# Seven block products for eight in the gate products of a fused attention and GLU kernel

## Chip, cores and metric

One core of one Trainium2 chip. The time is device microseconds (us) of one execution of the whole kernel; several runs are given by their median. Engines as the profile names them: PE is TensorE (matmuls), PEld its weight loads, DVE is VectorE, ACT is ScalarE, POOL is GpSimd, SP is SyncE, which issues most transfers. PSUM is the memory that PE writes to, in 8 banks; DVE and ACT read it, Pool does not. SBUF is the working memory.

## What is computed

Attention over chunks, chosen by bounds, for 4 batches of 8 heads, 768 positions and 64 dimensions; its output, laid out as 3072 tokens by 512, goes through a gated feed-forward layer (FFN) of 1536 columns:

```python
    # attention: for each query the top 6 chunks of 32 keys by an upper bound, causal
    scores = scale * np.matmul(q, k.transpose(0, 1, 3, 2))
    scores = np.where(mask, scores, -1000000000.0)
    ...
    attn = attn / (np.sum(attn, axis=-1, keepdims=True) + 1e-09)
    return np.matmul(attn, v).astype(np.float32)

    # FFN: x [3072, 512], w_gate and w_val [512, 1536], w_out [1536, 512]
    gate = 1.0 / (1.0 + np.exp(-(x @ w_gate)))
    val = x @ w_val
    return (gate * val @ w_out).astype(np.float32)
```

The sigmoid is computed as tanh of half the argument: (tanh(g/2) + 1) times v, with the factor 0.5 put in at the very end.

## The kernel before

The 3072 tokens are handled in eight units of 384 (`units`, u0 to u7), each of three blocks of 128 tokens. For each unit the kernel prepares keys and queries, bounds the chunks (`choose`, tiles `ub`, `ubn`, `mx`, `ap`, `apt`), computes scores (`sc`, L896), their exponentials on ACT (`exp`, L907), the causal mask on Pool (`cm`, L913), the product with the values (`pv`, L929), and turns the result into `xT`, a tile of 4 blocks of 128 input rows by 384 tokens. Then `ffn` (L1062) takes it through the FFN:

- 12 blocks of 128 FFN columns (`fb`). For each, a gate product `g` and a value product `v` (L1078): 4 matmuls each, one for each block of 128 input rows, that stream 384 tokens. ACT takes the tanh (`gate`, L1087) and DVE makes `hg` = (gate + 1) x v (L1091).
- Units 0 to 3 multiply `hg` by w_out as it is (`o`, L1119; `osb`, the output staging). Units 4 to 7 (`PAIRED`) do it in `pair` (L989): a product of 2 x 2 blocks by seven block products in place of eight (Strassen's scheme in Winograd's form), with sums of `hg` blocks (`sw`, `sx`, L1000) and of w_out blocks (`tw`, L984) on DVE and Pool, the products `p1` to `p7` (L1013) on PE, and sums out of PSUM on DVE (L1030). `held` keeps the third token block of an even unit until the odd unit's third block joins it (`u45`, `u67`).

Each step is added to a `Plan` by name, with its dependencies, the engines that may run it and an estimate of its cost. The order in which each engine gets its instructions, and which engine takes which step, is not decided when the kernel is built: it is written out in the string `ORDER` (`name=engine`, P for PE, A for ACT, V for DVE, G for Pool, S for SP), and the buffers in the string `SLOTS` (`name:slot`). Engines run their own instructions in that order; between engines only the dependencies hold. All PSUM tiles take one of 8 slots, so a product waits until the last reader of the former tile of its slot is done.

Loads of q, k, v go by SP's queue; w_gate (`wg0` to `wg2`), w_val (`wv`) and w_out (`wo`) go by Pool's queue, in thirds of 0.5 MB, between Pool's other instructions:

```python
    def weights(i, prio, after):
        lo, hi = 512 * i, 512 * i + 512
        return plan.add(f"wg{i}", {POOL: (760, 760)}, lambda e: nc.gpsimd.dma_start(wg16[:, :, lo:hi], wgs[:, :, lo:hi]),
                 reads=after, writes=[("wg", i)], prio=prio, dma=(3000, 2048)), ...
```

At the start, `first` handles block 0 of the batches (`kf`, `qf`, `vf`, `scf`, `attf`, `pvf`, `xf`, `xpsf`), `load_wide` brings the keys and queries of u1 and u2 (`kq_u`), and copies of a pattern (`epat`, steps `hkp`) fill parts of the key tiles `hk`.

Of the kernel before, what the change touches and what calls it, by code (L numbers as in the profile page):

```python
# [100 lines left out]
cmf_1_0=G k0_u1=S kn_u1_0=G kT_u1_0=P vf_1=S vf1_1=G vc_1=A pvf_1_0=P rzf_1_0=V xf_1_0=V vf1_2=G cmf_1_1=G xpsf_0_1=P pvf_1_1=P
rzf_1_1=V xf_1_1=V kf16_2=A scf_2=P xpsf_0_0=P xpsf_1_0=P ap0=V kx1_u1_2=V vf_2=S vc_2=A wg0=G wv0=G xpsf_1_1=P expf_2_0=A
cmf_2_0=G pvf_2_0=P ap1=V rzf_2_0=V kt_u1_0=V xf_2_0=V expf_2_1=A cmf_2_1=G pvf_2_1=P k1_u1=S q1_u1=S q2_u1=S qn_u1_2=A xTf_0_1=A
kn_u1_1=A kT_u1_1=P q0_u1=S k3_u1=S q3_u1=S qn_u1_1=G wv1=G kn_u1_3=G xTf_1_0=A xTf_0_0=A hkp110=A qn_u1_3=G xpsf_2_0=P qT_u1_2=P
hq1=V rzf_2_1=V xf_2_1=V xTf_1_1=V kx1_u1_0=V hk0_u1_0=V xpsf_2_1=P xTf_2_1=V kx1_u1_1=V wg1=G qn_u1_0=A xTf_2_0=A kt_u1_1=A
kcr_f=G wv2=G qf_u1_2=V qm_u1_2=G kT_u1_3=P qT_u1_1=P qf_u1_1=A hq1_u1_1=A kx0_u1_3=V qT_u1_3=P qf_u1_3=V kx1_u1_3=V qT_u1_0=P
qf_u1_0=V hk0_u1_2=G qm_u1_3=G kx0_u1_1=V kx0_u1_0=V kcr_u1=V hk1_u1_1=A qm_u1_1=A qm_u1_0=A wg2=G kt_u1_3=V hk1_u1_3=V hkf0=V
hq0_u1_2=V g_u0_3=P g_u0_0=P g_u0_2=P tanh_u0_3=A tanh_u0_2=A hq0_u1_3=A hkp101=A hq0_u1_0=A g_u0_1=P ub_u1=P ubn0_u1=V ubm0_u1=V
hq0=V mx0_u1=V ap0_u1=V apt0_u1=V hqm0_u1_0=G v_u0_0=P v_u0_2=P v_u0_3=P hg_u0_3=V wo0=G hkp111=G ubn1_u1=V tanh_u0_0=A hq0_u1_1=A
tanh_u0_1=A hg_u0_0=V v_u0_1=P hg_u0_1=V hg_u0_2=V v_u0_7=P v_u0_4=P hqm0_u1_2=A sc_u1_0_2=P exp_u1_0_2=A sc_u1_2_2=P sc_u1_2_0=P  # L110
sc_u1_0_1=P sc_u1_2_1=P exp_u1_0_1=A v_u0_5=P g_u0_5=P tanh_u0_5=A hq1_u1_0=V kcr1=V hk0_u1_3=V hg_u0_5=V g_u0_7=P tanh_u0_7=A
wo1=G hk0_u1_1=G hq1_u1_2=G hkf1=G hk1_u1_0=G hq1_u1_3=G exp_u1_2_1=A g_u0_4=P tanh_u0_4=A hg_u0_7=V ubm1_u1=V mx1_u1=V ap1_u1=V
apt1_u1=V sc_u1_3_2=P exp_u1_3_2=A exp_u1_2_2=A exp_u1_2_0=A cm_u1_2=G sc_u1_1_0=P sc_u1_1_2=P sc_u1_3_1=P exp_u1_1_2=A v_u0_6=P
sc_u1_0_0=P sc_u1_3_0=P g_u0_6=P exp_u1_3_1=A exp_u1_1_0=A tanh_u0_6=A exp_u1_3_0=A hg_u0_4=V hg_u0_6=V sc_u1_1_1=P v_u0_9=P
v_u0_8=P v_u0_10=P g_u0_10=P tanh_u0_10=A exp_u1_1_1=A hg_u0_10=V g_u0_9=P tanh_u0_9=A g_u0_11=P tanh_u0_11=A exp_u1_0_0=A
g_u0_8=P tanh_u0_8=A v_0_3=S wo2=G cm_u1_3=G hqm1_u1_2=G v_0_1=S v16_0_1=G v_0_2=S v16_0_3=G v16_0_2=G pv_u1_3=P pv_u1_2=P
# [242 lines left out]
def kernel(  # L359
# [10 lines left out]
    nc = tc.nc  # L370
# [19 lines left out]

    plan = Plan(
# [3 lines left out]
    )  # L395

# [665 lines left out]
    def ffn(u, base, span):  # L1062
# [4 lines left out]
        for fb in range(NFB):  # L1067
# [3 lines left out]
            if fb % 2 == 0:  # L1071
                hgs.append(Buf("hg", f"hg_{u.name}_{fb // 2}", [128, 2, T], F16))
# [185 lines left out]
```

## Time and profile before

| | us |
|---|---|
| median of 3 runs | 289.97 |
| lowest, highest | 289.52, 290.89 |
| the profiled execution, its own time | 288.62 |
| its span in the profile | 286.6 |

The span goes from the first to the last instruction that the profile records; the profiled execution's own time has what lies around it too. A row of the grouped views reads: line, engine, operation, what it writes <- what it reads, the shapes, the count | busy us, mean ns of one | idle time of the engine just before, and what ended it. In a timeline a row begins with start and length in us, and the bracket at its end is idle time of that engine before it with what released it. Matmuls are pipelined, so the length of one matmul overlaps the next; the distance of the starts is what it takes of PE.

Two more rows of the profile, its waits of the longest total (engine, line, what it waited for: us in total, times, longest):

```profile
ACT gate_u L1087 <- PE g_u L1078: 53.1, 44, 8.3
POOL sw L1000 <- DVE hg_u L1091: 30.8, 5, 8.2
```

### The profile page before, as it was taken

To read this page: it belongs to the slowest core of one execution; us is meant where nothing else is said; L and a number is where in the kernel's file an instruction comes from. 1 tells how busy PE (TensorE), PEld (TensorE's weight loads), DVE (VectorE), ACT (ScalarE), POOL (GpSimd) and SP (SyncE) were. 2 spreads that over 40 slices of the span, in tenths; PEclk is the share of its full clock that TensorE was granted. 3 is DMA by queue.
4 is the path that set the end of the run, shared out by engine and by line. 5 is a ranking of instruction groups with operands and counts; after the bars stand their busy time and mean duration, and the time that the engine had idled before them with its cause. 6 is when DMAs were issued, how large, how long until landed. Compare 5 with 4: busy or idle time off the path is not lost.

```text
span 286.6 us, 7277 instructions
## 1 busy us (share of the span) xinstructions
PE 272.8 (95%) x2764; PEld 186.3 (65%) x2764; DVE 212.3 (74%) x615; ACT 186.9 (65%) x392; POOL 148.2 (52%) x233
## 2 busy tenths in 40 slices
PE   3878999999999999999999999999999999999994
PEld 2654566667755765556677548767876786676673
DVE  3678846687999989796989997866725756373785
ACT  5688578779976965369999769997763402514210
POOL 6567773768394803926677765655611080130430
PEclk9999999999999999999999999999999999999999
DMA  7999999999999994799950030000020020000124
GB/s 166 238 221 195 196 204 223 249 174 204 175 206 188 163 193 104 160 162 243 173 113 2 0 113 2 2 0 2 2 77 0 1 75 0 2 0 0 68 81 183
DMA packets 123377, 32.69 MB, mean 114 GB/s; under 512 B 111440, under 2 KB 120400, under 8 KB 123344
## 3 DMA queue, kind: packets, MB, share of 16 engines
q1 hardware_dynamic: 118592, 27.53, 45.9%
q0 software_dynamic: 4752, 4.72, 9.8%
q8 instruction: 21, 0.34, 0.5%
q14 instruction: 12, 0.10, 0.1%
HBM read 30.67 MB, written 6.29 MB: 129 GB/s over the span
## 4 chain that ended last, share of the span: by engine, by line
PE 81%; DMA 12%; SPq 2%; POOL 1%; DVE 1%; issue 1%; DVEq 0%
PE g_u L1078 19%; PE v_u L1078 19%; PE sc_u L896 11%; PE o_u L1119 10%; PE p_u L1013 9%; PE pv_u L929 6%; DMA wo<-in_moe_w_out_dram 5%; DMA wg<-in_moe_w_gate_dram 4%; PE ube_u L835 2%; DMA kq_u<-in_q_dram 2%; PE xps_u L956 1%; SPq L586 1%; DMA kf<-in_k_dram 1%; SPq L575 1%; DVE ox L1030 1%
## 5 line engine op out<-in xcount | busy, mean ns | idle before, releaser
L907 ACT ACTIVATE att_u<-sc_u 128x512 f16<-128x512 f32 (+3 forms) x184 | 86.8, 570 | 5.0 <-PE sc_u L896 2.5
L1087 ACT ACTIVATE gate_u<-g_u 128x384 f16<-128x384 f32 x96 | 47.1, 503 | 58.4 <-PE g_u L1078 53.1
L1091 DVE SCALAR_TENSOR_TENSOR hg_u<-gate_u,v_u 128x384 f16<-128x384 f16 x96 | 50.8, 543 | 36.0 <-PE v_u L1078 20.9
L1078 PE MATMUL g_u<-xT_u,wg 128*128 128x384 f16 x384 | 73.2, 326 | 0.9 <-DMA wg<-in_moe_w_gate_dram 0.9
L1078 PE MATMUL v_u<-xT_u,wv 128*128 128x384 f16 x384 | 72.5, 326 | 0.0
L1078 PEld LDWEIGHTS <-wg 128*128 128x128 f16 x384 | 36.0, 98 | 24.5 <-DMA wg<-in_moe_w_gate_dram 1.8
L1078 PEld LDWEIGHTS <-wv 128*128 128x128 f16 x384 | 36.2, 98 | 22.9 <-issue 0.5
L913 POOL TENSOR_SCALAR_AFFINE_SELECT att_u<-att_u 128x384 f16<-128x384 f16 (+1 forms) x56 | 28.2, 514 | 36.1 <-ACT att_u L907 30.6
L1119 PE MATMUL o_u<-wo,hg_u 128*128 128x512 f16 x144 | 34.6, 379 | 0.4 <-DMA wo<-in_moe_w_out_dram 0.3
L929 PE MATMUL pv_u<-v,att_u 128*128 128x65 f16 x640 | 26.6, 193 | 0.0
L929 PEld LDWEIGHTS <-att_u 128*128 128x128 f16 x640 | 24.5, 98 | 2.2
L896 PE MATMUL sc_u<-hqo,hko 128*128 128x128 f16 (+2 forms) x220 | 25.7, 243 | 0.0
L896 PE MATMUL sc_u<-hqe,hke 128*128 128x128 f16 (+2 forms) x220 | 25.1, 243 | 0.0
L1119 PEld LDWEIGHTS <-hg_u 128*128 128x128 f16 x144 | 13.5, 98 | 13.9 <-issue 0.6
L612 POOL CAST v<-v 128x512 f16<-128x512 f32 x23 | 13.7, 613 | 15.0 <-DMA v<-in_v_dram 14.7
L896 PEld LDWEIGHTS <-hke 128*128 128x128 f16 x220 | 16.7, 98 | 5.3 <-ACT xT_u L407 0.6
L896 PEld LDWEIGHTS <-hko 128*128 128x128 f16 x220 | 16.2, 98 | 4.3 <-DVE hqo L409 0.2
L636 POOL TENSOR_SCALAR qm_u<-qf_u 128x768 f32<-128x768 f32 (+3 forms) x10 | 16.2, 1617 | 3.3 <-PE ubo_u L835 2.0
L1030 DVE SCALAR_TENSOR_TENSOR sw<-p_u,sw 128x256 f32<-128x256 f32 (+1 forms) x20 | 10.6, 529 | 6.1 <-PE p_u L1013 5.7
L948 DVE TENSOR_TENSOR x_u<-pv_u,rz_u 128x384 f16<-128x384 f32 (+1 forms) x28 | 14.5, 525 | 0.4
L858 DVE MAX8 mx_u<-ubn_u 128x8 f32<-128x8 f32 (+16 forms) x152 | 12.6, 159 | 0.3
L1128 ACT ACTIVATE osb_u<-o_u 128x512 f32<-128x512 f32 x10 | 6.0, 596 | 10.1 <-PE o_u L1119 10.1
(159 smaller groups left out, 442.5 us busy)
## 6 DMA issues: line engine op xcount, KB each, us to landing
v<-in_v_dram SPq DMA_DIRECT2D x23, 256.0 KB, 4.4
k<-in_k_dram SPq DMA_DIRECT2D x12, 384.0 KB, 5.5
q<-in_q_dram SPq DMA_DIRECT2D x12, 384.0 KB, 5.5
out_dram<-osb_u SPq DMA_DIRECT2D x12, 256.0 KB, 3.4
out_dram<-sw SPq DMA_DIRECT2D x8, 256.0 KB, 2.0
wg<-in_moe_w_gate_dram POOLq DMA_DIRECT2D x3, 512.0 KB, 11.5
wv<-in_moe_w_val_dram POOLq DMA_DIRECT2D x3, 512.0 KB, 11.2
wo<-in_moe_w_out_dram POOLq DMA_DIRECT2D x3, 512.0 KB, 13.2
```

Source lines behind the costliest of these rows:

```text
L612: plan.add(f"v16_{b}_{ib}", {POOL: pool(H * D)}, lambda e: nc.gpsimd.tensor_copy(v16[b % 2][:, ib, :, 0:D], at(t)), reads=[t], writes=[("v ...
L636: (nc.vector if e == DVE else nc.gpsimd).tensor_scalar_max(o, i, 0.0)
L896: nc.tensor.matmul(at(t)[:, o:o + 128 * m], hk[b % 2][e_][:, p, 128 * jb:128 * jb + 128], hq[u.side][e_][:, p, 128 * x:128 * (x + m)], sta ...
L907: plan.add(f"exp_{u.name}_{h}_{y}", {ACT: act(n)}, lambda e, t=t, att=att, b0=b0, n=n: nc.scalar.activation(at(att)[:, b0:b0 + n], at(t), ...
L913: nc.gpsimd.affine_select(out=dv, in_=dv, compare_op=ALU.is_ge, fill=0.0, base=0, pattern=[[0, u.m], [1, 128]], channel_multiplier=-1)
L929: nc.tensor.matmul(at(pv)[:, last, x, :], at(att)[:, c:c + 128], v16[b % 2][:, jb, h, :], start=(jb == 0), stop=(jb == ib))
L948: plan.add(f"x_{u.name}_{p}", {DVE: dve(u.t)}, lambda e: nc.vector.tensor_tensor(at(x_).rearrange("p a (e d) -> p e a d", e=2), at(pv)[:, ...
L1013: nc.tensor.matmul(at(to)[:, side], a(j)[:, i], b(j)[:, i], start=j == i == 0, stop=j == 2 and i == 1)
L1078: nc.tensor.matmul(at(t), w16[:, c, 128 * fb:128 * fb + 128], at(u.xt)[:, c, :], start=(c == 0), stop=(c == 3))
L1087: plan.add(f"tanh_{u.name}_{fb}", {ACT: act(T)}, lambda e, g=g, gate=gate: nc.scalar.activation(at(gate), at(g), AF.Tanh, scale=0.5), read ...
L1091: plan.add(f"hg_{u.name}_{fb}", {DVE: dve(T)}, lambda e, w_=w_, gate=gate, hg=hg, fb=fb: nc.vector.scalar_tensor_tensor(at(hg)[:, fb % 2], ...
L1119: nc.tensor.matmul(at(o), at(hgs[fc // 2])[:, fc % 2, 128 * tb:128 * tb + 128], wo16[:, fc, lo:hi], start=(fc == 0), stop=(fc == NFB - 1))
```

## The change

The gate products of units 5, 6 and 7 are changed for four of the six pairs of FFN column blocks: pairs 1 to 4, so blocks 2 to 9. A pair's product of 512 input rows by 256 columns with 384 tokens is cut into 2 x 2 blocks each way (input rows 256 + 256, columns 128 + 128, tokens 192 + 192) and done by seven block products for eight. Each block product is 2 matmuls of 192 tokens.

- `sums_of` adds, once for each pair, four sums of w_gate blocks (`ss0` to `ss3`, kept in slots of the `v` tiles) and, for each of the three units, four sums of `xT` blocks (`tt0` to `tt3`, kept in parts of the key and query tiles that are no longer needed).
- `by7` adds the seven products into four PSUM tiles (`p1`, `p26`, `p53`, `p74`), a move of `p1` to SBUF (`m1`), and six sums into two f32 tiles `f0` and `f1` of 384 tokens each, from which the tanh reads. For pairs 1, 3 and 4 (`SLOW7`) three moves (`m26`, `m53`, `m74`) first bring the products to SBUF (`tm`), so that the sums may run on Pool or DVE; for pair 2 the sums read PSUM and run on DVE. A moved tile takes one of two places in a key tile.
- Value products, the other gate products and the w_out products stay as they were.
- `ORDER` and `SLOTS` are new from their first entries; 24 of the 1826 steps go, 223 come, and 148 of the steps that stay run on another engine. In the plan, unit 5's FFN is added after unit 6's attention, and the estimates for `qm` on Pool are raised.

```diff
@@ ORDER, SLOTS @@
-ident=G v10=G ident16=V k2_u1=S kn_u1_2=A kT_u1_2=P epat0=V epat=G hkp010=V hkp011=A hkp100=A kcr0=V hkp000=G kf1_0=S kf0_0=S
...
+k2_u1=S ident=G epat0=V epat=G hkp010=A ident16=V hq1=V kcr0=V kn_u1_2=V kT_u1_2=P kt_u1_2=A kx1_u1_2=V kf1_0=S kf0_0=S kfT_0=P
...
@@ the planner's estimates of qm on Pool @@
-POOL: pool(2.2 * u.n)
+POOL: pool(3 * u.n)
-POOL: pool(4.6 * u.n)
+POOL: pool(6 * u.n)
@@ before ffn @@
+    SLOW7 = {(u, "g", i) for u in (5, 6, 7) for i in (1, 3, 4)}
+    BY7 = {u: {("g", i) for i in (1, 2, 3, 4)} for u in (5, 6, 7)}
...
+    def sums_of(u, next_):
...
+                w, out_ = blocks_of(m, i), ss[m, i]
+                for n, (a, b, op) in enumerate(((lambda w=w: w(1, 0), lambda w=w: w(1, 1), ALU.add), (out_[0][1], lambda w=w: w(0, 0), ALU.subtract),
+                                                (lambda w=w: w(0, 0), lambda w=w: w(1, 0), ALU.subtract), (lambda w=w: w(0, 1), out_[1][1], ALU.subtract))):
+                    plan.add(f"ss{n}_{m}{i}", {DVE: dve(256, 2), POOL: pool2(256)}, ...
...
+        for n, (a, b) in enumerate(((lambda: x_(0, 1), lambda: x_(0, 0)), (lambda: x_(1, 1), lambda: t_(0)),
+                                    (lambda: x_(1, 1), lambda: x_(0, 1)), (lambda: x_(1, 0), lambda: t_(1)))):
+            plan.add(f"tt{n}_{u.name}", {DVE: dve(384, 2), POOL: pool2(384)}, ...
...
+    def by7(u, m, i, next_, views):
...
+        f = [Buf("np", f"f{y}_{name}", [128, 2, 192]) for y in range(2)]
+        slow = (u.i, m, i) in SLOW7
...
+                for c in range(2):
+                    nc.tensor.matmul(at(to)[:, side], a()[:, c], b()[:, c], start=c == 0, stop=c == 1)
...
+        product("p1", p1, 0, lambda: w(0, 0), lambda: x_(0, 0), [])
+        product("p2", p26, 0, lambda: w(0, 1), lambda: x_(1, 0), [])
+        product("p6", p26, 1, s7[1][1], lambda: t_(1), tk(1))
+        product("p5", p53, 0, s7[0][1], lambda: t_(0), tk(0))
+        product("p3", p53, 1, s7[3][1], lambda: x_(1, 1), [s7[3][0]])
+        product("p7", p74, 0, s7[2][1], lambda: t_(2), tk(2))
+        product("p4", p74, 1, lambda: w(1, 1), lambda: t_(3), [(f"tt{u.i}", 3)])
...
+        def move(p, src, dst, n, reads, writes):
+            plan.add(f"{p}_{name}", {ACT: act(192 * n), DVE: dve(192 * n)}, lambda e: copy(e, dst(), at(src)), ...
+        move("m1", p1, lambda: v_(2), 1, [p1], [q[2]])
+        if slow:
+            tmp = Buf("tm", f"tm_{name}", [128, 3, 2, 192])
+            move("m26", p26, ...
+            move("m53", p53, ...
+            move("m74", p74, ...
...
+        def onto(p, n, src, dst, other, reads, writes):
+            plan.add(f"{p}_{name}", {POOL: pool2(192 * n), DVE: dve(192 * n)} if slow else {DVE: dve(192 * n)}, lambda e: both(e).tensor_tensor(
+                dst(), src[0](), other(), ALU.add), ...
+        onto("c11", 2, a26, lambda: v_(0, 2), lambda: v_(2).to_broadcast([128, 2, 192]), [q[2]], [q[0], q[1]])
+        onto("c4", 1, a5, lambda: v_(3), lambda: v_(1), [q[1]], [q[3]])
+        onto("c3", 1, a7, lambda: v_(2), lambda: v_(1), [q[1]], [q[2]])
+        onto("c12", 1, a3, lambda: v_(1), lambda: v_(3), [q[3]], [q[1]])
+        onto("c22", 1, a7, lambda: v_(3), lambda: v_(3), [q[3]], [q[3]])
+        onto("c21", 1, a4, lambda: v_(2), lambda: v_(2), [q[2]], [q[2]])
@@ ffn @@
+            seven = [u.i in BY7 and (m, fb // 2) in BY7[u.i] for m in "gv"]
...
+                if seven[0]:
+                    gs = by7(u, "g", fb // 2, next_, views)
...
+            if seven[0]:
+                _, gv, gk = gs[fb % 2]
+            else:
+                g = ps(f"g_{u.name}_{fb}", "ff", [128, T])
...
+            plan.add(f"tanh_{u.name}_{fb}", {ACT: act(T, not seven[0])}, lambda e, gv=gv, gate=gate: nc.scalar.activation(
+                at(gate), gv(), AF.Tanh, scale=0.5), reads=gk, writes=[gate], prio=next_(EV))
@@ the units' sequence @@
     attend(units[5], 5.0)
-    ffn(units[5], 6.0, 0.95)
...
     attend(units[6], 6.0)
+    ffn(units[5], 6.0, 0.95)
     ffn(units[6], 7.0, 0.95)
```

More of the change, by code (lines that the diff above doesn't have):

```diff
@@ L101 @@
[L101 to L104, printed above, removed]
```

576 lines of the change are left out of this document (334 added, 242 removed), and 2 rows, old and new, of the table plan.

## The prediction

> **What bounds the kernel now.** I read first the page's busy times and its row of granted clocks, then the busy time of each engine in four stretches (the columns are the stretch, its length, then each engine's busy us with its instructions in brackets, the granted clock, the DMA share and GB/s).
>
> ```profile
> span 286.6 us, 7277 instructions
> PE 272.8 (95%) x2764; PEld 186.3 (65%) x2764; DVE 212.3 (74%) x615; ACT 186.9 (65%) x392; POOL 148.2 (52%) x233
> ...
> PEclk9999999999999999999999999999999999999999
> ```
>
> ```profile
> 0.00:60.00 60.00, 50.70 (x466) 33.25 (x467) 40.49 (x127) 43.96 (x93) 38.23 (x71) 1.00 1.08 210
> 80.00:100.00 20.00, 20.00 (x193) 12.00 (x192) 19.16 (x56) 16.27 (x37) 14.83 (x22) 1.00 1.00 185
> 200.00:270.00 70.00, 70.00 (x613) 49.99 (x611) 39.71 (x101) 27.69 (x61) 19.59 (x32) 1.00 0.04 16
> 270.00:287.00 17.00, 12.10 (x99) 9.32 (x96) 11.55 (x27) 2.13 (x5) 3.98 (x6) 1.00 0.37 139
> ```
>
> PE is idle for 286.6 - 272.8 = 13.8 us, of which 60 - 50.70 = 9.3 us lie in the first 60 us and 17 - 12.10 = 4.9 us at the end. Between 200 and 270 us it has no gap while DVE is busy 57%, ACT 40% and Pool 28% of the time. A busy PE need not be PE at its peak, so next I took runs of equal matmuls out of the chain of waits (start, length, what):
>
> ```profile
> 206.49 0.91 PE pv_u L929 x30
> ...
> 217.56 1.95 PE v_u L1078 x12
> ...
> 228.06 2.62 PE p_u L1013 x24
> ```
>
> 384 columns take 1.95/12 = 162.5 ns, 256 take 109.2 ns, 65 take 30.3 ns: a straight line, 0.416 ns a column and 2.7 to 3.3 ns for each matmul. The page counts as many weight loads as matmuls, 2764 each, so a fresh load for every matmul is hidden even behind 65 columns. PE streams at its rate, and in this stretch only fewer columns, or a wait, can move the end. The timeline shows where it does wait late, and its last matmuls:
>
> ```profile
> 277.83 0.39 PE L1013 MATMUL p_u<-wo,held 128*128 128x256 f16 x2 [0.70 <-DVE held L409]
> ...
> 281.99 0.82 PE L1013 MATMUL p_u<-tw,hg_u 128*128 128x256 f16 x6
> ```
>
> One wait of 0.70 us, and 286.6 - 282.8 = 3.8 us for the last sums and store.
>
> **The change part by part.**
>
> *Fewer columns on PE.* Four pairs in each of three units are 12 pairs. Each loses 8 matmuls of 384 columns (8 x 162.5 = 1300 ns) and gets 7 products of 2 matmuls of 192 columns. No row shows 192; the line puts it between the 256 and the 65 columns at 162.5 - 192 x 0.416 = 82.6 ns, and 14 x 82.6 = 1156 ns. The saving is 144 ns a pair, 1.73 us in all. Nothing covers PE, so this counts in full if PE stays fed. The Trainium skill, "TensorE: Matmul & The Clock Gate", section "Back-to-back issue gap", speaks against it: it gives about 81 ns for a matmul of 128 columns and 131 ns for 512 in a real stream of loads and matmuls. On a line between these two, an estimate from that page, a pair would go from about 8 x 114 to 14 x 89 ns and the change would cost 4 us. The trace disagrees: 384 columns take 162.5 ns and 65 take 30.3 ns, each with its load.
>
> *What the other engines get.* Counted in the listing of the changed kernel: 27 two-block moves out of PSUM and 12 one-block moves, 72 sums, 16 weight sums (256 columns) and 12 input sums (384 columns). Of the 72 sums 28 stand on Pool and 44 on DVE, so "most on Pool" does not hold as listed. Prices:
>
> ```profile
> L1030 DVE SCALAR_TENSOR_TENSOR sw<-p_u,sw 128x256 f32<-128x256 f32 x12 | 5.1, 423 | 2.9 <-PE p_u L1013 2.5
> ...
> L1000 DVE TENSOR_TENSOR sw<-hg_u,sw 128x256 f16<-128x256 f16 x6 | 1.7, 282 | 0.0
> L409 DVE COPY qf_u<-qT_u 128x384 f32<-128x384 f32 x3 | 1.6, 546 | 0.4 <-PE qT_u L734 0.4
> ```
>
> ```profile
> L1087 ACT ACTIVATE gate_u<-g_u 128x384 f16<-128x384 f32 x96 | 47.1, 503 | 58.4 <-PE g_u L1078 53.1 <-DVE hg_u L1091 3.0 <-DVE ubn_u L851 1.7
> ```
>
> ```profile
> L636 POOL TENSOR_SCALAR qm_u<-qf_u 128x768 f32<-128x768 f32 x5 | 10.6, 2124 | 2.3 <-PE ubo_u L835 2.0 <-DVE qf_u L802 0.2
> ...
> L1000 POOL TENSOR_TENSOR sw<-sw,hg_u 128x256 f16<-128x256 f16 x5 | 3.4, 670 | 9.7 <-DVE sw L1000 9.6
> ...
> L984 POOL TENSOR_TENSOR tw<-wo,tw 128x512 f16<-128x512 f16 x2 | 2.3, 1152 | 0.0
> ...
> L627 POOL TENSOR_TENSOR kcr<-kx,kcr 128x96 f32<-128x96 f32 x3 | 1.3, 424 | 0.1
> ```
>
> DVE: 546 ns for 384 f32 and 423 for 256 give 0.96 ns a column, so 362 ns for 192. It gets 4 + 40 operations of that or the long size as sums (4 x 546 + 40 x 362 = 16.7 us), 9 long moves (4.9), 4 short ones (1.4), 9 weight sums (9 x 282 = 2.5) and 9 input sums (between 282 and 546 ns; nearer the f16 row, 360: 3.2): 75 instructions, 28.7 us. ACT: 18 long moves at the gate's 503 ns and 8 short ones at about 330 ns, 11.7 us. Pool: two f16 sizes give 188 ns and 1.88 ns a column, but the f32 rows give (424 - 188)/96 = 2.46 and (2124 - 188)/768 = 2.52; the sums are f32, so 192 columns cost 0.66 us and 384 cost 1.13. 8 long, 20 short, 7 weight sums at 0.67, 3 input sums at 0.91: 29.6 us.
>
> Against the stretch from 200 us to the end (about 87 - 1.7 = 85 us afterwards) DVE's 39.71 + 11.55 = 51.3 becomes some 76 us (about 4 us of the new sums stand earlier): 89%. Pool's 23.6 becomes some 53, ACT's 29.8 some 41. All this lies beside PE, and the row of 80 to 100 us shows that PE had no gap while DVE was busy 19.16 of 20 us and Pool 14.83. I cost it at nothing on average and take 0.5 us for new short waits, between a gain of 0.7 (the one wait above goes: the held copies now stand earlier or on ACT) and the loss of the first rival.
>
> *New waits.* A gate of a seven-product pair is no longer ready with its matmul: products, move, then three to six sums in a row, about 1.13 + 3 x 0.66 = 3.1 us on Pool before its tanh. In u6, ACT's tanh of block 8 waits for such a row; behind it in ACT's queue stand another tanh and the moves that empty two PSUM banks of pair 3; the next users of those banks are v of block 1 and the first product of u7's pair 1. So a late Pool sum comes back to PE by way of ACT and a bank. PE is given other products meanwhile, in an order that interleaves u5's, u6's and u7's blocks.
>
> *The start, searched anew.* All queues differ from their first entries. What ends the early idle time of PE:
>
> ```profile
> 4.98 1.46 POOL L411 COPY hke<-epat 64x1536 f16<-64x1536 f16 x1
> 9.55 0.61 POOL L612 CAST v<-vf 128x512 f16<-128x512 f32 x1 [3.11 <-DMA vf<-in_v_dram]
> ...
> 14.59 0.99 POOL L551 DMA_DIRECT2D wg<-in_moe_w_gate_dram  x1
> ```
>
> ```profile
> 23.30 2.77 PE L1078 MATMUL g_u<-xT_u,wg 128*128 128x384 f16 x16 [0.45 <-DMA wg<-in_moe_w_gate_dram]
> ...
> 33.38 0.82 PE L1078 MATMUL g_u<-xT_u,wg 128*128 128x384 f16 x4 [0.47 <-DMA wg<-in_moe_w_gate_dram]
> ```
>
> The first gate load is issued from Pool's queue when Pool gets to it, not when a landing allows it. In the new order two more copies of 1.46 us, one cast of 0.61 and no copy of 0.50 stand ahead of it: 3.0 us more, of which the wait of 3.11 us for v takes up two copies. What is left over is about 0.1, and up to 1.1 us if one copy falls behind that wait; the first gate matmul at 23.30 is late by as much. The loads that follow no longer stand behind query copies in Pool's queue, which can take away the 0.47 at 33.38. On SP's queue the wide key and query loads of u1 change places, the same bytes. I take 0, between -1 and +1.5 us.
>
> *Sum.* 286.6 - 1.73 + 0.5 + 0 = 285.4 us of span. The profiled run took 288.62 us, 2.0 around its span, so 287.4; the runs' median, 289.97, lies 1.35 above it: 288.7 us.
>
> **The rivals.**
>
> *DVE and Pool fall behind, and PE waits (slower).* Place: from the first block product on, where the listing has 166 DVE instructions, 61 with two operands in SBUF, against 73.5 us of PE columns (its matmuls in the listing at the rates above).
>
> ```profile
> 275.68 0.67 POOL L1000 TENSOR_TENSOR sx<-held,sx 128x256 f16<-128x256 f16 x1 [0.69 <-DVE held L409]
> 275.71 0.78 DVE L1000 TENSOR_TENSOR sx<-hg_u,hg_u 128x256 f16<-128x256 f16 x1
> 276.30 0.72 POOL L1000 TENSOR_TENSOR sx<-held,hg_u 128x256 f16<-128x256 f16 x1
> 276.52 0.64 DVE L1000 TENSOR_TENSOR sx<-sx,held 128x256 f16<-128x256 f16 x1
> ```
>
> A DVE sum of 282 ns took 780 when it began 0.03 us after a Pool sum, and ended 0.14 us after it: it sat out the whole of it. With Pool busy two thirds of this stretch (its 67 instructions there at the prices above make 48 us), 61 such sums that lose half a Pool sum (0.33 us) two times in three make 13 us on an engine with about 9 to spare, so 4 to 5 us come out on PE: 289.97 - 1.73 + 4.7 = 292.9. It decides once the collisions cost more than those 9 us. For it: the rows above. Against it: many of Pool's sums would have to run just when DVE's do, and the row of 80 to 100 us. The Trainium skill, "SBUF — State Buffer", section "Who interferes with whom", states this lock outright: a DVE instruction with two SBUF inputs and a Pool instruction that reads SBUF exclude each other for a whole instruction; the trace agrees, 0.78 against 0.28 us.
>
> *The start gives the gain away.* The first gate load goes out 1.1 us later and nothing later makes it up: 288.7 + 1.1 = 289.8, no change.
>
> *The new order also fills idle time.* 9.3 us early and 0.7 late are there to be had; 1.5 of them, without the 0.5 of new waits, make 288.7 - 2.0 = 286.7. For it: the loads that stand freer in Pool's queue. Against it: most of the early gaps wait for transfers of the same size.
>
> *Weight loads bound the short matmuls.* The page's loads last 98 ns; if 192 columns could not hide one, a pair would take 14 x 98 = 1372 ns instead of 1300, 0.9 us more in all: 291.3. The 65-column row is against it.
>
> ```profile
> L929 PEld LDWEIGHTS <-att_u 128*128 128x128 f16 x640 | 24.5, 98 | 2.2
> ```
>
> **How the numbers follow.** Forecast 0.42, the start 0.16, DVE and Pool 0.20, filled idle time 0.20, weight loads 0.02. The first is 288.7 us, by its own bounds 288.0 to 289.6. A measurement here tells 0.5% from no change, 1.45 us, so faster means below 288.5 and slower above 291.4. The forecast sits at that line: half its chance below. Faster 0.21 + 0.20 = 0.41; same 0.21 + 0.16 + 0.02 and a few hundredths of DVE and Pool falling behind mildly, 0.41; slower 0.18. The range runs from 286.7, the filled case, to 292.2, most of the way to the slow one.
>
> **What would show it.** Right: the products' matmuls 82 to 83 ns apart, PE without gaps from 60 us to the last 20, DVE near 90% after 200 us, the span some 1.2 us shorter, the first gate matmul within 1 us of 23.3. Wrong: idle PE after 200 us released by ACT's moves or DVE's sums (the first rival, by its length), DVE sums on f32 in SBUF well over 362 ns, or early idle time other than 9.3 us by more than 1. Pool's 192-column sums at 0.59 or less would mean I priced f32 too high.

## The result, and the profile after

The changed kernel takes 291.76 us (median of 19 runs, 290.72 to 293.63), the kernel before 289.49 in the runs beside them: ratio 1.0075, 95% interval 1.0057 to 1.0093. It is slower by about 2.2 us, where 288.7 was forecast.

The profiled execution of the changed kernel took 293.28 us, near the top of its 19 runs, and that of the kernel before 288.62, near the bottom of its own. So the two spans lie 5.0 us apart where the medians lie 2.3. For this reason a second profile of the changed kernel (run e18 below, 290.70 us, span 289.0) stands beside the first. First the page of the changed kernel, then busy time in the four stretches of the prediction.

```profile
span 291.6 us, 7584 instructions
...
PE 274.1 (94%) x2836; PEld 192.1 (66%) x2836; DVE 245.0 (84%) x692; ACT 193.5 (66%) x414; POOL 174.3 (60%) x273
...
PEclk9977999999999999999999999999999999999999
```

```profile
0.00:60.00 60.00, 49.96 (x448) 33.66 (x456) 38.64 (x115) 39.43 (x84) 39.80 (x72) 0.94 1.04 206
80.00:100.00 20.00, 20.00 (x184) 11.94 (x183) 18.41 (x58) 16.47 (x36) 13.32 (x20) 1.00 0.87 174
200.00:270.00 70.00, 68.27 (x711) 54.21 (x709) 63.45 (x156) 37.67 (x88) 41.97 (x63) 1.00 0.09 32
```

The same stretches of the second profile:

```profile
0.00:60.00 60.00, 50.46 (x462) 34.04 (x463) 39.52 (x117) 40.59 (x87) 40.26 (x73) 0.91 1.07 210
80.00:100.00 20.00, 20.00 (x200) 12.22 (x198) 18.17 (x56) 16.75 (x37) 13.81 (x21) 1.00 0.90 174
200.00:270.00 70.00, 68.28 (x697) 53.90 (x695) 63.85 (x156) 38.73 (x92) 43.98 (x66) 1.00 0.08 32
```

What both profiles share is what to explain. Between 200 and 270 us PE, which had no gap before, is idle for 70 - 68.27 = 1.73 us (1.72 in the second), and DVE is busy 91% of the time instead of 57%. The first 60 us differ by more between the two profiles of one kernel (0.5 us of busy time and 0.03 of granted clock) than one could read a cause from.

The saving itself is there. A run of products in the chain of waits:

```profile
247.59 2.31 PE p_g_u L1148 x28
```

2.31/28 = 82.5 ns for 192 columns; 82.6 was forecast. Summed over PE's matmuls at their undisturbed distances, the work is 1.77 us less than before. The groups of instructions show what the sums cost:

```profile
L1185 DVE TENSOR_TENSOR f_g_u<-hke,f_g_u 128x192 f32<-128x192 f32 x18 | 8.4, 482 | 0.1
L1185 DVE TENSOR_TENSOR f_g_u<-p_g_u,f_g_u 128x192 f32<-128x192 f32 x15 | 5.1, 351 | 0.2
L1185 DVE TENSOR_TENSOR f_g_u<-hko,f_g_u 128x192 f32<-128x192 f32 x7 | 4.7, 673 | 0.1
...
L1185 POOL TENSOR_TENSOR f_g_u<-hko,f_g_u 128x192 f32<-128x192 f32 x13 | 7.7, 604 | 1.5 <-ACT gate_u L1228 1.0
...
L1185 POOL TENSOR_TENSOR f_g_u<-hke,f_g_u 128x384 f32<-128x384 f32 x4 | 4.1, 1031 | 3.8 <-DVE hke L435 2.1 <-ACT hke L433 1.5 <-ACT f_g_u L433 0.2
```

The same sum of 192 columns on DVE takes 351 ns when one operand comes from PSUM, and 482 or 673 on average when both come from SBUF. The timeline shows why, and how it reaches PE:

```profile
220.48 1.13 POOL L1185 TENSOR_TENSOR f_g_u<-hko,f_g_u 128x384 f32<-128x384 f32 x1
...
220.66 1.17 DVE L1185 TENSOR_TENSOR f_g_u<-hke,f_g_u 128x192 f32<-128x192 f32 x1
221.75 0.34 DVE L1185 TENSOR_TENSOR f_g_u<-p_g_u,f_g_u 128x192 f32<-128x192 f32 x1
222.02 0.54 DVE L1237 SCALAR_TENSOR_TENSOR hg_u<-gate_u,v_u 128x384 f16<-128x384 f16 x1
...
222.61 0.81 PE L1216 MATMUL v_u<-xT_u,wv 128*128 128x384 f16 x4 [0.53 <-DVE hg_u L1237]
```

A DVE sum begins 0.18 us after a Pool sum of 384 columns and sits it out: 1.17 us for 0.35. The `hg` queued behind it empties a PSUM slot 0.8 us late, and the next value product on PE waits 0.53 us for that slot. Counted over the 26 DVE sums of pairs 1, 3 and 4: 12 of them ran while a Pool instruction ran, and took 0.736 us on average; of the 14 others, 13 are of 192 columns and took 0.350 (the one of 384 took 0.552). `hg`, with one operand in PSUM, takes 0.55 us in both cases. Against the shortest of their size, these sums lose 4.8 us of DVE's time behind 196 us, the weight sums and the sums of `hg` blocks together 4.6, and the input sums 1.6: 11.0 us in all (9.9 in the second profile). The sums of `hg` blocks are no part of the change; they lose 1.6 us in the kernel before.

The last place is the middle, where few steps of the change stand (sums of weight blocks and moved casts, no block product). The stretch from 130 to 145 us, first in the kernel before, then in the two profiles of the changed kernel, and the first profile's timeline there:

```profile
130.00:145.00 15.00, 15.00 (x183) 10.02 (x182) 11.25 (x31) 13.49 (x30) 10.42 (x14) 1.00 1.08 218
...
130.00:145.00 15.00, 13.49 (x161) 8.96 (x159) 12.42 (x33) 11.74 (x27) 9.21 (x13) 1.00 0.82 165
...
130.00:145.00 15.00, 14.68 (x174) 9.76 (x173) 13.54 (x36) 11.93 (x28) 10.56 (x16) 1.00 0.89 179
```

```profile
132.97 0.82 POOL L437 CAST k<-k 128x768 f16<-128x768 f32 x1 [5.96 <-DMA k<-in_k_dram]
133.74 0.61 POOL L638 CAST v<-v 128x512 f16<-128x512 f32 x1
134.42 0.82 POOL L437 COPY hko<-kt 64x768 f16<-64x768 f16 x1
135.32 1.37 POOL L939 TENSOR_SCALAR_AFFINE_SELECT att_u<-att_u 128x384 f16<-128x384 f16 x2
...
136.15 0.46 PE L955 MATMUL pv_u<-v,att_u 128*128 128x65 f16 x9 [1.51 <-POOL att_u L939]
```

In the new order a cast of keys that have not landed stands at the head of Pool's queue for 6 us. The causal masks behind it are late, and PE waits 1.51 us for them. In the second profile the same cast waits 4.73 us, and PE only 0.28 us for the masks.

### The profile page after: what moved, and what is told of

Read it like the earlier page. It is cut to its first block, busy times and chain, and to the rows that moved or that the text cites. A ratio compares the mean times of both kernels' runs of the same rounds, so it can differ in the third digit from the quotient of the medians.

```text
span 291.6 us, 7584 instructions
## 1 busy us (share of the span) xinstructions
PE 274.1 (94%) x2836; PEld 192.1 (66%) x2836; DVE 245.0 (84%) x692; ACT 193.5 (66%) x414; POOL 174.3 (60%) x273
## 5 line engine op out<-in xcount | busy, mean ns | idle before, releaser
L1216 PE MATMUL v_u<-xT_u,wv 128*128 128x384 f16 x384 | 73.9, 326 | 1.2 <-DVE hg_u L1237 0.8
L1216 PE MATMUL g_u<-xT_u,wg 128*128 128x384 f16 x288 | 57.8, 333 | 2.3 <-DMA wg<-in_moe_w_gate_dram 2.3
L1228 ACT ACTIVATE gate_u<-g_u 128x384 f16<-128x384 f32 x72 | 35.4, 499 | 33.9 <-PE g_u L1216 29.6
L1216 PEld LDWEIGHTS <-wg 128*128 128x128 f16 x288 | 26.9, 99 | 20.3 <-issue 3.4
L1265 PE MATMUL o_u<-wo,hg_u 128*128 128x512 f16 x144 | 33.5, 379 | 0.0
L955 PE MATMUL pv_u<-v,att_u 128*128 128x65 f16 x640 | 27.6, 193 | 1.7 <-POOL att_u L939 1.5
L955 PEld LDWEIGHTS <-att_u 128*128 128x128 f16 x640 | 25.1, 98 | 5.2 <-POOL att_u L939 1.6
L1228 ACT ACTIVATE gate_u<-f_g_u 128x384 f16<-128x384 f32 x24 | 12.0, 521 | 10.2 <-DVE f_g_u L1185 5.2
L1185 POOL TENSOR_TENSOR f_g_u<-hke,f_g_u 128x192 f32<-128x192 f32 (+1 forms) x11 | 8.4, 768 | 10.1 <-DVE f_g_u L1185 5.4
L1185 POOL TENSOR_TENSOR f_g_u<-hko,f_g_u 128x192 f32<-128x192 f32 (+1 forms) x17 | 11.9, 709 | 4.0 <-ACT f_g_u L433 2.5
L812 DVE STREAM_TRANSPOSE kt<-k 128x768 f16<-128x768 f16 x12 | 11.5, 962 | 2.6 <-POOL k L437 2.5
```

The lines of the kernel that those rows point to most:

```text
L955: nc.tensor.matmul(at(pv)[:, last, x, :], at(att)[:, c:c + 128], v16[b % 2][:, jb, h, :], start=(jb == 0), stop=(jb == ib))
L1185: plan.add(f"{p}_{name}", {POOL: pool2(192 * n), DVE: dve(192 * n)} if slow else {DVE: dve(192 * n)}, lambda e: both(e).tensor_tensor(dst( ...
L1216: nc.tensor.matmul(at(t), w16[:, c, 128 * fb:128 * fb + 128], at(u.xt)[:, c, :], start=(c == 0), stop=(c == 3))
L1228: plan.add(f"tanh_{u.name}_{fb}", {ACT: act(T, not seven[0])}, lambda e, gv=gv, gate=gate: nc.scalar.activation(at(gate), gv(), AF.Tanh, s ...
L1265: nc.tensor.matmul(at(o), at(hgs[fc // 2])[:, fc % 2, 128 * tb:128 * tb + 128], wo16[:, fc, lo:hi], start=(fc == 0), stop=(fc == NFB - 1))
```

## The experiments

Each ratio is to the kernel before in the same group of runs on the same chip; groups ran on different chips, so only ratios are compared, and they differ from the quotients of the medians by up to 0.3%. "Start" is the order up to about 85 us (628 steps), "middle" from there to about 204 us, "tail" the rest; a seam is the step where one kernel's order is joined to the other's. "Sums on Pool" are the 26 sums of pairs 1, 3 and 4 that the change gives to DVE; `x_u7_0` is DVE's copy of the last attention block out of PSUM.

| run | start, middle, tail | ratio | 95% interval |
|---|---|---|---|
| changed kernel, 19 runs | new, new, new | 1.0075 | 1.0057 to 1.0093 |
| e18, the same again | new, new, new | 1.0072 | 1.0046 to 1.0097 |
| e1 | old, new, new | 1.0046 | 1.0021 to 1.0071 |
| e2 | old, old, new (bad seam) | 1.0179 | 1.0137 to 1.0222 |
| e3 | new, old, old | 1.0046 | 1.0011 to 1.0081 |
| e4 | all new, PE's early gaps filled | 1.0053 | 1.0028 to 1.0078 |
| e5 | old, old, new | 1.0024 | 1.0001 to 1.0048 |
| e6 | new, new, old | 1.0114 | 1.0083 to 1.0145 |
| e7 | all old, gaps filled | 1.0010 | 0.9988 to 1.0032 |
| e8 | all new, sums on Pool | 1.0020 | 0.9995 to 1.0045 |
| e9 | old, old, new with sums on Pool, x_u7_0 first (bad seam) | 0.9991 | 0.9959 to 1.0023 |
| e10 | all new, moves on ACT | 1.0087 | 1.0052 to 1.0121 |
| e11 | as e8, x_u7_0 first | 0.9991 | 0.9960 to 1.0023 |
| e12 | all new, weights loaded sooner | 1.0037 | 1.0005 to 1.0068 |
| e13 | as e9, the seam mended | 0.9940 | 0.9910 to 0.9970 |
| e14 | e11, e12 and e15 together | 1.0005 | 0.9978 to 1.0032 |
| e15 | all new, a cast moved | 1.0127 | 1.0088 to 1.0167 |
| e16 | new, then as e13 | 0.9969 | 0.9945 to 0.9993 |
| e17 | old, new, tail as e13 | 0.9992 | 0.9966 to 1.0018 |

### Start, middle or tail

In e1, e2 and e3 the order string is cut at one step and joined to the other kernel's:

```diff
@@ ORDER of the changed kernel: e1 (cut after 628 steps), e2 (after 1363) @@
-k2_u1=S ident=G epat0=V epat=G hkp010=A ident16=V hq1=V kcr0=V kn_u1_2=V
+ident=G v10=G ident16=V k2_u1=S kn_u1_2=A kT_u1_2=P epat0=V epat=G
...
@@ ORDER of the kernel before: e3 (cut after 628 steps) @@
-ident=G v10=G ident16=V k2_u1=S kn_u1_2=A kT_u1_2=P epat0=V epat=G
+k2_u1=S ident=G epat0=V epat=G hkp010=A ident16=V hq1=V kcr0=V kn_u1_2=V
...
```

> The changed kernel with the first 628 steps of its order (to about 85 us) taken from the kernel before, with the buffers that they had there; everything behind is as changed, block products included; nothing is left out. Theory 1, the start lost the gain (by 32 us the changed kernel's PE is 2.9 us behind in the two profiles): 291.8 - 2.9 = 288.9 us, first gate matmul near 23.3 us, granted clock 1.00. Rival, the loss is behind 85 us (DVE's and Pool's sums, the wait of 1.5 us at 134): 291.8 us.

> The changed kernel with the first 1363 steps of its order (to about 203 us) from the kernel before; only the last part, with nearly all the block products and their sums, is as changed; nothing is left out. By theory 1 and the waits seen behind 200 us (about 2 us in the changed kernel's profile) the tail is worth -1.7 + 2 = about 0: 289.5 to 290 us. Rival, the collisions of DVE and Pool are the whole loss: 289.5 + 2.3 = 291.8. Had the tail given what was forecast for it (-1.73 + 0.5): 288.3.

> The kernel before, without any block product, with the first 628 steps of its order taken from the changed kernel: the start alone. Theory 1: 289.5 + 2.9 = 292.4 us, granted clock below 1.00 as in the changed kernel. Rival, the start is free and the loss comes with the block products: 289.5 us.

e1 gives back 0.29% (0.8 us), not the 1.0% that the two first profiles suggested, and e3 costs 0.46%. So the start is worth some 0.8 to 1.3 us by these two, with intervals nearly as wide, and e1 leaves 1.3 behind it. e2 is no evidence on the tail: the weight sums `ss`, which the new order spreads over the middle, all fell behind the seam, and PE has 10 - 7.14 = 2.9 us of idle time there that neither kernel has (its windows):

```profile
200.00:210.00 10.00, 7.14 (x104) 6.06 (x104) 9.65 (x29) 6.94 (x16) 5.32 (x8) 1.00 0.01 2
```

e5 mends that; e6 is its mirror.

```diff
@@ e5: the order of the kernel before up to its step 1376, then the changed order; in the first part: @@
+ss0_g3=V ss0_g1=V tw0_1=V ss0_g2=G ss0_g4=V ss1_g2=V ss1_g3=V ss1_g1=G ss3_g3=V ss2_g1=V
...
@@ e6: the changed order up to its step 1386 without them, then the order of the kernel before @@
-ss0_g3=V ss0_g1=V ss0_g2=G ss0_g4=V ss1_g2=V ss1_g3=V ss1_g1=G ss3_g3=V ss2_g1=V
```

> As e2_only_tail, but the seam mended: the order of the kernel before up to about 204 us, with the weight sums (ss) and four other small steps put where the changed order has them, and then the changed order; nothing is left out. Theory 2, the waits behind 200 us (2.9 us there in the changed kernel's profile against 0.9 before) eat what the products save (1.73): 289.5 - 1.73 + 2.0 = 289.8 us. Rival, all that e1 left is the tail's: 290.8. Forecast of the prediction for this part alone (-1.73 + 0.5): 288.3.

> The mirror of e5: the changed order up to about 204 us, without its weight sums, and then the order of the kernel before, with no block product anywhere. Theory 2 (the tail is worth nothing, the new order of start and middle costs it all): 291.5 us. Rival, the start's 1.2 us of e3 are all and the tail costs the rest: 290.7 us.

e5: the new tail alone costs 0.24% (289.5 x 1.0024 = 290.2), between theory 2's 289.8 and the rival's 290.8; both lie in the interval. The forecast for this part, 288.3, does not. It still has PE's waits of the changed kernel behind 215 us, 0.51 us for `hg` in the first of them, beside 0.7 us of idle time at the seam (its row from 145 to 200 us, below, reads 54.32). The products' saving and the tail's waits about cancel. e6, the new start and middle without any block product, costs 1.14%. That is more than the whole change, and more than theory 2 gave it (291.5, which is 0.7%); six runs, and a seam of its own, make its size weak, but it shows that a loss comes without any block product.

```profile
145.00:200.00 55.00, 54.32 (x701) 37.94 (x699) 49.52 (x165) 47.27 (x97) 39.87 (x54) 1.00 0.06 17
```

### The clock at the start

In the first profile of the changed kernel ten gate matmuls run while the granted clock is one half (the view of stretches, 16 to 32 us, mean clock 0.79; before 1.00).

```profile
16.00:32.00 16.00, 12.07 (x96) 7.39 (x97) 10.96 (x39) 11.13 (x24) 9.19 (x14) 0.79 1.17 213
```

```diff
@@ e4: the changed kernel; e7: the kernel before, with 10, 4, 15 and 6 at pvf_2_0, pvf_2_1, qT_u1_3, g_u0_3 @@
+    FILL = {"xpsf_1_1": 8, "pvf_2_0": 16, "pvf_2_1": 6, "g_u0_0": 30}
+    def fill(o, n, turn=False):
+        for _ in range(n):
...
+                nc.tensor.matmul(o, ident16, ident16, start=True, stop=True)
```

> The changed kernel with 60 matmuls of 128 columns of the identity added on PE where it idles between 16 and 25 us (8, 16, 6 and 30, each into a PSUM tile that the next matmul overwrites), so that the granted clock does not fall to half at 18 and 25 us; the order is as changed, nothing is left out. Theory 1a, the fallen clock is what most of the start's loss is (10 gate matmuls at 320 ns for 162: 1.6 us): 291.8 - 1.6 = 290.2 us. Rival 1b, the late first gate load and later transfers set the pace, and a faster PE only waits longer for them: 291.8 us, the clock at 1.00 all the same.

> The kernel before with 35 matmuls of 128 columns of the identity added on PE where it idles between 17 and 23.5 us (10, 4, 15 and 6), nothing else changed. Theory 3: the fallen clock costs the kernel before too (in its 29 runs the span goes with the granted clock, 286.5 us where that is 0.99 or more, 288.1 where it is less): the clock is then near 1.00 in nearly every run and the median 289.5 - 1.2 = 288.3 us. Rival: the clock only shows how long PE waited, and filling changes nothing: 289.5 us.

The filled matmuls do keep the clock up: its mean over a run is 1.00 in the median of both. Without them it is 0.986 in the changed kernel, and 0.991 in the runs of the kernel before beside e7. But e7 takes as long as the kernel before (1.0010), and e4's ratio is 0.2% below the changed kernel's, within the intervals. In the 29 runs of the kernel before that stood beside e1 to e4 a lower clock does go with a longer span (0.99 and above: 286.5 us in 8 runs; below: 288.1 in 21). In the 29 beside e7 the same split gives 286.5 and 287.0 us, so a gain of 0.2 us or so could hide in e7's interval; one of 1.2 us, theory 3's, could not. Both kernels have the same median clock, 0.986, and the second profile of the changed kernel has more time at half clock than the first (10.24 us against 6.83) and the shorter span. So the fallen clock is not what the change lost. That it is only a sign of idle PE fits this, but no run shows it.

The Trainium skill, "TensorE: Matmul & The Clock Gate", section "Part 1: The HAM clock gate (the "warmup" mystery)", tells of a half-rate state after idle stretches of some 3.4 us. The traces show that length (two stretches of 3.41 us in the first profile, one of three times as much in the second), but not the idle stretch: PE's longest idle time between 8 us and the first of them, at 18.3 us, is 1.18 us. The page's count of the cost, throttled time times the share of lost clock, would give e7 some 2.6 us (an estimate from it: 0.009 of 287 us), and the runs give none.

### DVE's late sums

```diff
@@ e8: ORDER, 26 such steps at their places @@
-c4_g1_u5=V
+c4_g1_u5=G
...
@@ e10: ORDER of the changed kernel, 13 such steps @@
-m53_g4_u5=V
+m53_g4_u5=A
...
```

> The changed kernel with the 26 sums of pairs 1, 3 and 4 that run on DVE moved to Pool, at the same places of the order; nothing is left out. Theory 4, DVE is late behind 200 us because its sums with two SBUF operands sit out Pool's (482 and 673 ns for 351): without them the waits on hg go and 1 to 1.5 us come back: 290.5 us. Rival 4b, DVE is merely full, so any relief helps as much, but Pool (16 us more, chains of 1.05 + 5 x 0.6 = 4 us) is now late for tanh: 293 us or more.

> The changed kernel with the 13 moves out of PSUM that run on DVE moved to ACT, same places of the order; nothing is left out. DVE gets 9 x 0.55 + 4 x 0.34 = 6.3 us less, half of what e8 took from it, but all its 26 two-operand sums still run beside Pool's. Theory 4b (DVE is merely full): the waits behind 200 us halve, from 3.3 to about 2.2 us, ratio 1.0075 - 0.004 = 1.0035. Theory 4 (the collisions): less than 0.5 us of it comes back, ratio 1.006 or more. A third way, ACT is late with its tanh instead: 1.009 or more.

e8 gives back 0.55%, 1.6 us, as theory 4 had it (289.27 measured, 290.5 expected on a chip where the kernel before took 289.5). Its groups and the stretch behind 200 us:

```profile
L1185 POOL TENSOR_TENSOR f_g_u<-hke,f_g_u 128x192 f32<-128x192 f32 x25 | 15.3, 627 | 0.9 <-ACT hke L433 0.3
...
L1185 DVE TENSOR_TENSOR f_g_u<-p_g_u,f_g_u 128x192 f32<-128x192 f32 x15 | 5.0, 351 | 0.3
```

```profile
200.00:270.00 70.00, 69.68 (x724) 55.46 (x722) 56.81 (x139) 39.70 (x94) 56.35 (x88) 1.00 0.08 32
```

DVE falls from 63.45 to 56.81 us of 70, Pool rises from 41.97 to 56.35, and PE's idle time falls from 1.73 to 0.32. Pool's longer chains do not show on PE, against rival 4b. e10 came out the third way. Some old waits are gone, but ACT is now late with moves on which PSUM slots hang (its timeline), and PE is idle for more than before:

```profile
213.37 0.33 PE L1148 MATMUL p_g_u<-xT_u,wg 128*128 128x192 f16 x2 [0.55 <-ACT f_g_u L433]
217.09 1.46 PE L1216 MATMUL g_u<-xT_u,wg 128*128 128x384 f16 x8 [1.13 <-ACT f_g_u L433]
218.85 0.33 PE L1148 MATMUL p_g_u<-hke,ss_g 128*128 128x192 f16 x2 [0.30 <-ACT hko L433]
```

So the runs do not part the collisions from a DVE that is merely full. e8 took 26 sums off DVE and, with them, their collisions; but the two-operand sums that stayed on DVE, those of w_out included, still lose some 8 us behind 196 us in e8's trace, where they lose 6 to 7 in the changed kernel's two, and PE hardly waits for them. e10 left all 26 sums where they were, and two of the five waits of PE on DVE that the first profile has behind 200 us are gone, 0.53 and 0.36 us; but PE's new waits on ACT come ahead of them and may hide them. What the trace does show is that 4.8 of the 14 us that the 26 sums took on DVE were time sat out, and the one chain above, from a collision to a wait of PE. The Trainium skill, "SBUF — State Buffer", section "Who interferes with whom", names the lock; the rows above agree, the instruction with a PSUM operand that is spared among them.

### The first weights, and the middle

```diff
@@ e11: e8, and @@
-k16_2_2=G kt_2_2=V
...
+k16_2_2=G k16_2_0=G kt_2_2=V kt_2_0=V
...
-rz_u7_0=V sw1_u45_1=V x_u7_0=V
+rz_u7_0=V x_u7_0=V sw1_u45_1=V
@@ e12: the changed kernel @@
-hkp000=G cmf_1_1=G vc_1=G vf1_2=G cmf_1_0=G wg0=G wv0=G
+cmf_1_1=G vc_1=G vf1_2=G cmf_1_0=G wg0=G wv0=G hkp000=G
@@ e15: the changed kernel, POOL's order and the turn on DVE that reads the cast @@
-k16_3_1=G v16_1_4=G hk1_2_1=G cm_u4_1=G cm_u4_7=G
+v16_1_4=G hk1_2_1=G cm_u4_1=G cm_u4_7=G k16_3_1=G
...
```

> As e8 (changed order, the 26 sums on Pool), with two more steps moved: on Pool the key cast that waits for its load at 127 to 133 us goes behind the two causal masks that PE's 1.0 to 1.7 us wait at 134 us is for, and x_u7_0 goes first on DVE as in e9; nothing is left out. Theory 5 (the middle's loss is that cast at the head of Pool's queue): 0.9 us of the middle and 0.5 of the tail come back, ratio 1.002 - 0.005 = 0.997. Rival, the late keys then hold up the scores that need them and the wait only moves: 1.000 to 1.002.

> The changed kernel with one copy of 1.46 us (hkp000) moved from ahead of the first gate and value loads on Pool's queue to behind them; nothing is left out. If the first gate load's issue sets the start (it goes out at 15.40 us in the changed kernel, 14.59 before), it goes out at about 13.9, the first gate matmul comes 1 to 1.5 us earlier, and the start's 1.2 us come back: ratio 1.0035. Rival, the transfers are full from 4 us on and an earlier weight only holds back keys and queries: 1.0075.

> The changed kernel with one key cast on Pool (k16_3_1, batch 3) moved behind the masks cm_u4_1 and cm_u4_7 that stood behind it, and the key turn on DVE that reads it (kt_3_1) moved five steps back; e11 had moved another cast (batch 2) that does not wait. Nothing is left out. Theory 5: PE's wait at 134 us (1.5 to 1.7 us in the changed kernel's profile, 0.6 to 1.0 in others) goes, ratio 1.0075 - 0.0045 = 1.003. Rival, the batch's keys are late for the scores that follow and the wait only moves: 1.006 to 1.0075.

e11 moved the wrong cast: that of batch 2, while the one that waits is of batch 3. So it says nothing on the middle. It is 0.29% below e8, with overlapping intervals; of that the trace explains 0.1%, the wait of 0.32 us on PE for `x_u7_0` that is gone. e12 gives back 0.38%, as the start theory had it, but its interval overlaps that of the changed kernel, and its first gate load goes out at 14.59 us instead of 15.40, so 0.8 us sooner, not the 1.5 expected. e15 moved the right cast: the wait at 134 us is gone, and another has come at 142 us, ahead of scores; the profile puts it down to an `hg` on DVE.

```profile
142.37 1.34 PE L976 MATMUL sc_u<-hqe,hke 128*128 128x128 f16 x9 [0.60 <-DVE hg_u L1291]
```

PE's idle time from 130 to 145 us is 0.81 us, between the 1.51 and 0.32 of the changed kernel's two profiles, and its ratio, 1.0127 in six runs, is no better; it lies above the rival's 1.006 to 1.0075 too. The wait moved, as the rival had it. That late keys are why, and that the cast is what the middle loses by, is not shown.

### A version that beats both, and the parts one by one

```diff
@@ e9, e13: order of the kernel before to its step 1376, then the changed order, with e8's 26 steps on Pool and x_u7_0 first @@
-c4_g1_u5=V
+c4_g1_u5=G
...
@@ e9 alone: behind the seam @@
+ss1_g2=V ss1_g3=V ss3_g3=V ss2_g1=V
@@ e14: the changed order with the edits of e8, e12, e15, and x_u7_0 first @@
```

> The order of the kernel before to about 204 us, then the changed order (as e5, with PSUM slots and four weight sums at the seam placed so that nothing waits there), the 26 sums of e8 on Pool, and DVE's copy-out of the last attention block (x_u7_0) ahead of a long input sum; nothing is left out. If theories 2 and 4 hold together, the products' 1.77 us remain and the waits behind 200 us are no more than before's (about 1 us): ratio to the kernel before 0.993, some 2 us less. Rival, something of the tail's loss is neither collision nor order (its longer chains, the clock): ratio 0.998 to 1.002.

> As e9 (order of the kernel before to about 204 us, then the changed order, 26 sums on Pool, x_u7_0 first), but the weight sums stay where e5 had them; e9 had put four of them behind the seam, where DVE then came 2.7 us late for PE at 203 to 210 us; nothing is left out. If theories 2 and 4 hold together, the products' 1.77 us are now seen: ratio 0.993. Rival, the weight sums cost PE their time wherever they stand: 0.998 or more.

> The changed order from end to end, with what the runs point to: hkp000 behind the first weight loads (e12), the waiting cast of Pool moved (e15), the 26 sums on Pool (e8), x_u7_0 first (e11); nothing is left out. If the costs add, 1.0075 - 0.0038 (e12) - 0.0084 (e11) - 0.003 (middle): ratio 0.992 to 0.994. If the start's gain was chance (its interval was 0.6% wide), 0.996; if the middle only moves its wait, 0.9965.

e9 had a fault of its own: four weight sums at its seam made DVE late, and PE waited 1.11 us at 208 us.

```profile
209.68 0.39 PE L1093 MATMUL p_u<-wo,sw 128*128 128x256 f16 x2 [1.11 <-DVE sw L1080]
```

e13 has them back at their places, and is faster than the kernel before: ratio 0.9940, medians 287.90 and 289.35 us. Its page and its stretches:

```profile
span 284.9 us, 7580 instructions
...
PE 272.0 (95%) x2836; PEld 191.8 (67%) x2836; DVE 232.7 (82%) x659; ACT 197.0 (69%) x420; POOL 192.1 (67%) x300
```

```profile
130.00:145.00 15.00, 15.00 (x186) 10.13 (x185) 11.07 (x33) 13.49 (x30) 10.42 (x14) 1.00 1.04 210
145.00:200.00 55.00, 55.00 (x720) 38.82 (x718) 50.35 (x167) 48.05 (x99) 40.13 (x55) 1.00 0.10 22
200.00:270.00 70.00, 69.52 (x680) 54.15 (x677) 57.78 (x137) 37.27 (x89) 57.93 (x91) 1.00 0.08 32
```

0.60% is 1.74 us, the size of the products' saving, with 0.9 us of uncertainty to either side: with the old start and middle and the sums on Pool, about all of it is kept. e14 has the new start and middle, and all that was forecast to mend them; it stays at 1.0005, so the moves of e12 and e15 add nothing to e11. e16 to e18 ask for each part alone.

```diff
@@ e16: e13 with the changed order's first 628 steps @@
-ident=G v10=G ident16=V k2_u1=S kn_u1_2=A kT_u1_2=P epat0=V epat=G
+k2_u1=S ident=G epat0=V epat=G hkp010=A ident16=V hq1=V kcr0=V kn_u1_2=V
...
@@ e17: e1 with e8's 26 steps on Pool, x_u7_0 first @@
-c4_g1_u5=V
+c4_g1_u5=G
...
```

> The kernel of e13 (ratio 0.994) with its first 628 steps, to about 85 us, taken from the changed order: what the changed start costs by itself. Nothing is left out. Theory 1 (e3: 1.2 us): ratio 0.998. Rival, the start costs nothing and e3's 0.46% was the seam or chance: 0.994.

> The start of the kernel before to about 85 us, and then the changed order with its tail mended as in e13 (26 sums on Pool, x_u7_0 first): against e13 only the middle, 85 to 204 us, is as changed. Nothing is left out. Theory 6, the changed middle costs 1 to 1.5 us (PE's waits at 134 and 187 to 192 us): ratio 0.998. Rival, it costs nothing: 0.994.

> The changed kernel itself once more, for the same chip and the same runs of the kernel before as e16 and e17. Taken as parts that add, e13's 0.994, the start of e16, the middle of e17 and the unmended tail (e8: 0.0055): 0.994 + 0.004 + 0.004 + 0.0055 = 1.0075, as in its 19 runs. Rival, the parts do not add and the chips differ: up to 1.011, as e6 and e15 had.

e17 against e13 differs in the middle alone: 0.52%, 1.5 us, the intervals just overlapping. Its stretches show part of it as idle PE, 0.76 and 0.29 us where e13 has none:

```profile
130.00:145.00 15.00, 14.24 (x171) 9.52 (x170) 13.18 (x35) 12.50 (x29) 9.21 (x13) 1.00 0.87 174
145.00:200.00 55.00, 54.71 (x684) 37.68 (x682) 50.84 (x162) 46.05 (x93) 37.67 (x53) 1.00 0.14 30
```

Four pairs of runs differ in each part alone, but for the seams:

| part | pairs | cost |
|---|---|---|
| start | e16 to e13, e3 to before, changed to e1, e11 to e17 | 0.29, 0.46, 0.29, 0.00% |
| middle | e17 to e13, e11 to e16, e6 to e3, e1 to e5 | 0.52, 0.22, 0.68, 0.22% |
| tail, sums on DVE and not on Pool | changed to e8, e1 to e17, e18 to e11, e5 to e13 | 0.55, 0.54, 0.81, 0.84% |

(All but the first pair of the tail also differ in `x_u7_0`, and e11 has a second cast moved.) The tail's cost is 1.6 to 2.4 us, and in each of its pairs the two intervals lie apart. The middle's is 0.6 to 2.0 us, 1.2 on average; only e6 and e3 lie apart, by a hair, but the idle PE is there in every profile: the twelve with the new middle have 0.3 to 1.8 us between 130 and 200 us, the kernel before and those with the old middle none, but for two bad seams. The start's is 0.75 us on average, and no pair lies apart. Together: -1.74 + 0.75 + 1.2 + 2.0 = 2.2 us, and 2.2 were measured. This sum is no proof by itself: the steps from e13 to e17, to e1 and to the changed kernel add up to it whatever they are; the other pairs are the check.

## Why the prediction was wrong, step by step

- *Fewer columns on PE, 1.73 us.* Right: 82.5 ns for 192 columns, 1.77 us less work, and 1.74 us (0.9 to 2.6) in e13.
- *What the other engines get.* The prices held where nothing ran beside: 350 ns for a DVE sum of 192 columns (362 forecast), 604 to 627 on Pool (660). DVE at 91% between 200 and 270 us looks like the 89% forecast behind 200 us, but it holds 9.5 us of time sat out, which the forecast left to a rival; without it DVE would be at 77%. "I cost it at nothing on average and take 0.5 us for new short waits" was the first step that failed. With 26 sums on DVE the tail's waits cost 1.6 to 2.4 us. The row of 80 to 100 us, on which the step leaned, did not carry over: there a DVE busy 96% cost PE nothing, behind 200 us one busy 91% did.
- *The first rival* had this mechanism and its place. It put the sums' lost time at 13 us, and 11.0 were measured; it then let 4 to 5 us come out on PE, and about 2 did. Its condition, collisions above the 9 us that DVE has to spare, was met in size, but DVE had more to spare than that and was still 9% idle on average: it was late at single places. Whether collisions or DVE's load made it late there is open, but for the one chain shown.
- *The middle.* The sum has no term for the order between 60 and 200 us; the forecast's sign "PE without gaps from 60 us to the last 20" was taken for granted, though all orders are new and the middle too got new steps on DVE and Pool. This is the second step that failed, and it is an omission: the new order costs about 1.2 us there (0.6 to 2.0). What in it costs this stays open. The cast that waits ahead of the masks is one place of idle PE, but e15, which moved it, won nothing.
- *The start: "I take 0, between -1 and +1.5 us".* It costs about 0.75 us, inside the bounds, and not clear of noise in any one pair. The first gate load goes out at 15.2 to 16.2 us with the new start (e12 and e14 apart), 13.9 to 14.6 with the old; the first gate matmul does not follow it from profile to profile: 23.4 to 25.1 us with the new start, 22.8 to 26.0 with the old.
- *The rivals of filled idle time and of bounding weight loads* did not come about; 82.5 ns excludes the latter.
- The time lies inside the range of 286.7 to 292.2, at its far end, and in part by luck: that end was drawn for the first rival alone, which explains the tail's 2 us, while the middle and the start, which had no term or a zero, make up the rest. The direction was wrong, a gain of 1.2 us forecast and a loss of 2.2 measured; the chance of slower, 0.18, was too low because the forecast looked for new waits only where the block products stand.

## What to carry to other kernels

When a change comes with a newly searched order, cost the order as an edit of its own, over the whole span: put the part that is wanted into the old order, and see whether the rest of the new one pays. Here the wanted part was worth about 1.7 us, and the order around it cost more. On an engine with two-operand sums in SBUF next to a busy Pool, average free time says little: look for the single late result that a PSUM slot hangs on. Here it paid to give the 26 sums to Pool, 1.6 us or more.

## What the runs showed that was not expected

- The granted clock at the start changes from run to run in one and the same kernel (0.976 to 1.000 on average over a run), and the changed kernel's two profiles have 6.83 and 10.24 us at half clock. Keeping it up with filled matmuls brought the kernel before nothing that was measured (1.0010, 0.9988 to 1.0032).
- A DVE sum with both operands in SBUF can take three times its time beside Pool (1.17 us for 0.35); `hg`, with one operand in PSUM, loses nothing (0.55 us in both cases).
- In e8 Pool is loaded to 80% (56.35 of 70 us) with chains of up to six sums before a tanh, and no wait of PE there is put down to it.
